# Two layer norms in a row as one function, in a two-layer attention and MLP kernel with its backward pass

## The chip, the cores and the metric

The kernel runs on one core of a Trainium2 chip. The metric is the device time of one execution in microseconds (us); lower is better. A core has five engines that run side by side: PE (TensorE, matmuls and transposes), DVE (VectorE), ACT (ScalarE), POOL (GpSimd) and SP (SyncE, which here issues most loads). They wait for each other through semaphores. Data moves between HBM and the core's memories on 16 DMA engines.

## The reference

Forward pass of four blocks over a state `x` of shape 2 x 1 x 1024 (batch 2, one token), and the gradient of all inputs but `B_x`. The weights are shared by the two layers.

```
_layernorm(x): (x - mean) / sqrt(var + 1e-5)

x = x + A(_layernorm(x))     # attention: q = y @ wq, 32 query heads, 4 kv heads, a cache
                             # of 16384 keys and values of 128, softmax, @ wo
x = x + B(_layernorm(x))     # B(x): y = _layernorm(x); gelu(y @ w1 + b1) @ w2 + b2
x = x + A(_layernorm(x))
x = x + B(_layernorm(x))
outputs: x, and d/d(x, k_cache, v_cache, wq, wo, w1, b1, w2, b2) for a given grad_out
```

B normalizes its input again, so the input of each MLP goes through two layer norms in a row: y1 = LN(x), y2 = LN(y1). wq is 1024 x 4096, wo 4096 x 1024, w1 1024 x 3584, w2 3584 x 1024; k_cache and v_cache hold 2 x 4 x 16384 x 128 bf16 values each.

## The kernel before

**Layout.** A state vector lies as `[128, 8, 2]` (1024 = 8 x 128, and the batch of two), so a layer norm sums first along the free dimension on DVE and then over the 128 partitions with a PE matmul against a matrix of ones (`part_sum`, L187 to L190). The order of the work is written out by hand in the kernel's code; each engine runs its own instructions strictly in that order.

**Loads.** Weights and cache come in tiles of 1 MB, `[128, 4096]` bf16, into a pool `ld` of seven buffers. SP issues a load when the buffer it goes to has been read to the end; SP's loads stand in one queue, in program order.

**Forward MLP** (`mlp_hidden`): `ln_fwd` twice, a copy to bf16 (`m_all`), then `w_fwd` over w1 (L337, into the PSUM bank `ACCT`), then gelu. `ln_fwd` takes the power -0.5 on POOL (L225).

**Backward MLP** (`weights_down`, for layer 1 and then layer 0). It multiplies by w1 transposed, goes backward through the two layer norms, and multiplies by wo transposed:

- `Back` is a product with a transposed weight. Some rows of the weight (the first `nd` blocks of 128) are turned on DVE (`turn32`, L269) and multiplied by `products` (L296) into a bank `..._d`; the others are turned on PE in *units* of eight 128 x 128 transposes (`turn`, L358, tiles `wtp` in a PSUM pool of two) with one copy by ACT back over the weight (L159), and multiplied at L418 into a bank `..._p`. `columns` (L305, L308) turns the `_d` bank into columns `_f`. `banks` takes both banks from the pool `ps_x` of four and clears them on DVE (L394, L397), `open` spreads the input gradient over the partitions with PE (`spg`, L278) and DVE (L281), `run` goes through the eight tiles, `some(k, n)` emits n units of tile k.
- In `weights_down`, `w1b` (banks `dm_d`, `dm_p`) is followed by `wob` (banks `do_d`, `do_p`). Seven loads of wo are emitted at once; the eighth, and SP's loads behind it, wait until the product of wob's first tile (L418 `do_p`) has released a buffer. While the layer norms run backward, PE is given units of wob's first two tiles, eight units in all, emitted through the hooks of `ln_bwd`: `hook` stands ahead of the partition sum, `after` behind it.

```
        wob.banks()
        dn = ln_bwd(dm[:], sv["y2"][:], sv["rstd2"][:], "dn", lambda: None, lambda: some(2))
        dx = ln_bwd(dn[:], sv["y1"][:], sv["rstd1"][:], "dx", lambda: some(2), lambda: some(3))
        ...
        wob.open(gA_all[:, 0:DJ, lsl(l)])
        some(8)
        wob.run()
```

So PE's order is: partition sum `lb_ps`, four units, partition sum, three units, `spg`, one unit, then the products.

**Around it.** `weights_down(1)` is followed by the attention backward of layer 1; `weights_down(0)` by the last stage, in which all gradients of the caches and weights are made and stored (`kv_pair` L1336, `dw_units` L1250, stores issued by POOL at L1213, loads by SP at L1282). `ACCT` is not in use during `weights_down`.

Of the kernel before, what the change touches and what calls it, by code (L numbers as in the profile page):

```python
# [10 lines left out]
F32 = mybir.dt.float32  # L11
I32 = mybir.dt.int32
ACT = mybir.ActivationFunctionType
ALU = mybir.AluOpType
# [5 lines left out]
LN_EPS = 1e-5  # L20
# [3 lines left out]
def kernel(  # L24
# [25 lines left out]
    V = nc.vector  # L50
# [3 lines left out]
    B, _, D = A_x.shape  # L54
# [6 lines left out]
    DJ = D // 128  # L61
# [14 lines left out]
    WIDE = 32  # L76
# [17 lines left out]
    def pt(shape, dtype, name):  # L94
        return ps_tp.tile(shape, dtype, name=name, tag="tp")

    def px(shape, dtype, name):
        return ps_x.tile(shape, dtype, name=name, tag="x")

    def pa(shape, dtype, name):  # L100
        return ps_acc.tile(shape, dtype, name=name, tag="acc")
# [31 lines left out]
    ACCT = pa([128, 512], F32, "acc_all")  # L133
# [11 lines left out]
    def copies_on(e):  # L145
        only["e"] = e
        load["A"] = load["D"] = 0.0
# [25 lines left out]
    def bcast_j(ap2, J):  # L173
        return ap2.unsqueeze(1).to_broadcast([128, J, 2])
# [12 lines left out]
    def part_sum(src, n, name):  # L187
        ps = pm_([128, n], F32, name)
        PE.matmul(ps[:], lhsT=onesf[:], rhs=src, start=True, stop=True)
        return ps  # L190
# [15 lines left out]
            V.tensor_copy(out=row[:, j0 * 128:(j0 + 4) * 128], in_=ps[0:2, :, :].rearrange("p a b -> p (a b)"))  # L206
        queue.dma_start(dram_out, row[:, :])

    def ln_fwd(xT, name):
        s1 = small.tile([128, 2], F32, name="ln_s1")  # L210
        V.tensor_reduce(out=s1[:], in_=xT.rearrange("p j b -> p b j"), axis=AX.X, op=ALU.add)
        ps = part_sum(s1[:], 2, "ln_ps")
        negmu = small.tile([128, 2], F32, name="ln_negmu")
        V.tensor_scalar(out=negmu[:], in0=ps[:], scalar1=-1.0 / D, scalar2=None, op0=ALU.mult)
        xc = wrk.tile([128, DJ, 2], F32, name="ln_xc")
        V.tensor_tensor(out=xc[:], in0=xT, in1=bcast_j(negmu[:], DJ), op=ALU.add)
        sq = wrk.tile([128, DJ, 2], F32, name="ln_sq")
        V.tensor_tensor(out=sq[:], in0=xc[:], in1=xc[:], op=ALU.mult)
        s2 = small.tile([128, 2], F32, name="ln_s2")
        V.tensor_reduce(out=s2[:], in_=sq[:].rearrange("p j b -> p b j"), axis=AX.X, op=ALU.add)  # L220
        ps2 = part_sum(s2[:], 2, "ln_ps2")
        vpe = small.tile([128, 2], F32, name="ln_vpe")
        V.tensor_scalar(out=vpe[:], in0=ps2[:], scalar1=1.0 / D, scalar2=LN_EPS, op0=ALU.mult, op1=ALU.add)
        rstd = vec.tile([128, 2], F32, name=name + "_rstd")
        nc.gpsimd.tensor_tensor(out=rstd[:], in0=vpe[:], in1=neghalf[:], op=ALU.pow)  # L225
        y = vec.tile([128, DJ, 2], F32, name=name + "_y")
        V.tensor_tensor(out=y[:], in0=xc[:], in1=bcast_j(rstd[:], DJ), op=ALU.mult)
        return y, rstd

    def ln_bwd(dy, y, rstd, name, hook=lambda: None, after=lambda: None):  # L230
        t1 = wrk.tile([128, DJ, 2], F32, name="lb_t1")
        V.tensor_tensor(out=t1[:], in0=dy, in1=y, op=ALU.mult)
        s = small.tile([128, 2, 2], F32, name="lb_s")
        V.tensor_reduce(out=s[:, 0, :], in_=dy.rearrange("p j b -> p b j"), axis=AX.X, op=ALU.add)
        V.tensor_reduce(out=s[:, 1, :], in_=t1[:].rearrange("p j b -> p b j"), axis=AX.X, op=ALU.add)
        hook()
        ps = part_sum(s[:].rearrange("p a b -> p (a b)"), 4, "lb_ps")
        after()
        nm = small.tile([128, 2, 2], F32, name="lb_nm")
        V.tensor_scalar(out=nm[:].rearrange("p a b -> p (a b)"), in0=ps[:], scalar1=-1.0 / D, scalar2=None,  # L240
                        op0=ALU.mult)
        u = wrk.tile([128, DJ, 2], F32, name="lb_u")
        V.tensor_tensor(out=u[:], in0=y, in1=bcast_j(nm[:, 1, :], DJ), op=ALU.mult)
        V.tensor_tensor(out=u[:], in0=u[:], in1=dy, op=ALU.add)
        V.tensor_tensor(out=u[:], in0=u[:], in1=bcast_j(nm[:, 0, :], DJ), op=ALU.add)
        dx = wrk2.tile([128, DJ, 2], F32, name=name, tag="lb_dx")
        V.tensor_tensor(out=dx[:], in0=u[:], in1=bcast_j(rstd, DJ), op=ALU.mult)
        return dx
# [112 lines left out]
    class Back:  # L361
# [26 lines left out]
                if self.todo[k]:  # L388
                    self.todo[k].popleft()()

        def banks(self):
            if self.nd:
                self.acc = px([128, 512], F32, self.name + "_d")
                V.memset(self.acc[:, 0:32 * self.nd], 0.0)  # L394
            if self.np:
                self.p = px([128, self.np, WIDE], F32, self.name + "_p")
                V.memset(self.p[:], 0.0)  # L397

        def open(self, gT):
            self.gT = gT  # L400
# [383 lines left out]
    def cols4(J, name, used=True):  # L784
        t = vec.tile([128, J + 7, 4], BF16, name=name)
        V.memset(t[:, (J if used else 0):J + 7, :], 0.0)
        return t[:]
# [5 lines left out]
    m_all = cols4(DJ, "m_all")  # L793
# [5 lines left out]
    saved = {}  # L799
    ALLG = list(range(G))  # L800

    def lsl(l):
        return slice(2 * l, 2 * l + 2)
# [18 lines left out]
        return xn  # L822

    def mlp_hidden(l, xT):
        y1, rstd1 = ln_fwd(xT[:], f"m{l}a")
        y2, rstd2 = ln_fwd(y1[:], f"m{l}b")
        V.tensor_copy(out=m_all[:, 0:DJ, lsl(l)], in_=y2[:])
        hps = w_fwd(B_w1, D, F, m_all[:, 0:DJ, lsl(l)])
        hpre = vec.tile([128, FJ, 2], F32, name=f"hpre{l}")
        V.tensor_tensor(out=hpre[:], in0=hps, in1=b1T[:].to_broadcast([128, FJ, 2]), op=ALU.add)  # L830
        x2 = wrk.tile([128, FJ, 2], F32, name="g_x2")
        V.tensor_tensor(out=x2[:], in0=hpre[:], in1=hpre[:], op=ALU.mult)
        w_ = wrk.tile([128, FJ, 2], F32, name="g_w")
        V.tensor_scalar(out=w_[:], in0=x2[:], scalar1=GELU_A, scalar2=1.0, op0=ALU.mult, op1=ALU.add)
        u = wrk.tile([128, FJ, 2], F32, name="g_u")
        V.tensor_tensor(out=u[:], in0=w_[:], in1=hpre[:], op=ALU.mult)
        z = wrk.tile([128, FJ, 2], F32, name="g_z")
        S.activation(out=z[:], in_=u[:], func=ACT.Exp, scale=2.0 * GELU_C)
        V.tensor_scalar(out=z[:], in0=z[:], scalar1=1.0, scalar2=None, op0=ALU.add)
        rz = wrk.tile([128, FJ, 2], F32, name="g_rz")  # L840
        V.reciprocal(out=rz[:], in_=z[:])
        th = vec.tile([128, FJ, 2], F32, name=f"th{l}")
        V.tensor_scalar(out=th[:], in0=rz[:], scalar1=-2.0, scalar2=1.0, op0=ALU.mult, op1=ALU.add)
        hh = wrk.tile([128, FJ, 2], F32, name="g_hh")
        V.tensor_scalar(out=hh[:], in0=th[:], scalar1=1.0, scalar2=0.5, op0=ALU.add, op1=ALU.mult)
        V.tensor_tensor(out=h_all[:, 0:FJ, lsl(l)], in0=hh[:], in1=hpre[:], op=ALU.mult)
        saved[f"m{l}"] = dict(y1=y1, rstd1=rstd1, y2=y2, rstd2=rstd2, hpre=hpre, th=th, xT=xT)

    def mlp_out(l, fps):
        xn = vec.tile([128, DJ, 2], F32, name=f"xM{l}")  # L850
# [25 lines left out]
    def weights_down(l, gT, name, mid=None):  # L876
        sv = saved[f"m{l}"]
        w1b = Back(B_w1, D, F, 4, [1, 0, 3, 2, 5, 4, 6], "dm")
        for k in range(len(w1b.tiles)):
            w1b.load(k)  # L880
        w1b.banks()
        w1b.open(dh_all[:, 0:FJ, lsl(l)])
        copies_on("A")
        w1b.some(0)
        w1b.run(mid)
        wob = Back(A_wo, HD, D, 16, [4, 5, 0, 1, 6, 2, 3, 7], "do")
        for k in range(NLD):
            wob.load(k)
        w1b.columns()
        dm = wrk.tile([128, DJ, 2], F32, name="dm_sb")  # L890
        for (p, ap), e in zip(w1b.parts(), (V.tensor_copy, S.copy)):
            e(out=dm[:, p], in_=ap)
        q = deque([(0, 0), (0, 0), (0, 0), (0, 0), (1, 0), (1, 0), (1, 0), (1, 0)])

        def some(n):
            for _ in range(n):
                if q:
                    wob.some(q.popleft()[0], 1)

        wob.banks()  # L900
        dn = ln_bwd(dm[:], sv["y2"][:], sv["rstd2"][:], "dn", lambda: None, lambda: some(2))
        dx = ln_bwd(dn[:], sv["y1"][:], sv["rstd1"][:], "dx", lambda: some(2), lambda: some(3))
        gn = vec.tile([128, DJ, 2], F32, name=f"gM{l}")
        V.tensor_tensor(out=gn[:], in0=dx[:], in1=gT[:], op=ALU.add)
        V.tensor_copy(out=gA_all[:, 0:DJ, lsl(l)], in_=gn[:])
# [3 lines that stand above are left out]
        wob.columns()  # L909
        copies_on(None)  # L910
        return gn, wob.parts()
# [174 lines left out]
    banks = {"tp": lambda: pt([128, 8, 128], BF16, "tpe")}  # L1086
# [423 lines left out]
    m = 0  # L1510
    while 2 * m < NS + 2:
# [7 lines left out]
        for k in range(2):  # L1519
            s = 2 * m + k  # L1520
            if s < NS:
                i, b = NCH + s // NB, s % NB
# [97 lines left out]
```

## Time and profile before

| | |
|---|---|
| time, median of 3 runs | 1140.46 us (1137.77 to 1141.27) |
| profiled execution: its own time / its span | 1139.88 us / 1138.1 us |
| busy, of the span: PE, DVE, ACT, POOL | 80%, 54%, 47%, 6% |
| moved by DMA | 449.20 MB, mean 395 GB/s |
| layer norms of `mlp_hidden`, from the first reduction to `m_all` | 207.1 to 214.2 us (layer 0), 428.3 to 435.7 us (layer 1) |
| `weights_down` from `dm_sb` to the first `do_p` product | 468.8 to 477.4 us (layer 1), 709.8 to 718.4 us (layer 0) |

Positions are us from the start of the span. In the stage tables ("windows"), the columns after the stretch are its length, then busy time and number of instructions of PE, PEld (weight loads), DVE, ACT and POOL, then the granted PE clock (1.00 is full speed), the busy share of the 16 DMA engines, and GB/s. In the chain of waits, each piece is what the piece after it waited for.

### The profile page before, as it was taken

How to read it: one execution, taken by the hardware profiler on the slowest of the kernel's cores; microseconds unless marked ns; L12 is line 12 of the kernel's file. 1: busy time of each engine (PE TensorE's matmuls, PEld its weight loads, DVE VectorE, ACT ScalarE, POOL GpSimd, SP SyncE). 2: the span in 40 equal slices, each digit the busy share in tenths (PEclk: the TensorE clock that was granted, in tenths of full speed). 3: DMA queues.
4: the chain of work that ended last, by engine and by line, in shares of the span. 5: the costliest groups of instructions: out<-in, count | busy, mean ns of one | idle time of the engine just before them, and what ended most of it. 6: DMA issues, size and time to landing. Idle time of an engine off the chain costs nothing.

```text
span 1138.1 us, 38123 instructions
## 1 busy us (share of the span) xinstructions
PE 915.9 (80%) x16766; PEld 674.7 (59%) x16767; DVE 619.8 (54%) x1363; ACT 534.0 (47%) x1356; POOL 70.2 (6%) x124
## 2 busy tenths in 40 slices
PE   4979795468888975789887678888898897899996
PEld 3867674358766754778765567755545454455552
DVE  1545451180545523654442246678798767786876
ACT  0544351005544420434333214468697766676764
POOL 0000000000000000000000000022121111111210
PEclk9988895567999875899998678999999978897978
DMA  8999999999999979999999699998999999999997
GB/s 371 423 425 425 424 424 413 395 413 423 423 425 423 412 288 404 388 422 421 399 413 393 232 380 309 370 386 302 403 419 421 421 419 424 423 411 421 423 385 290
DMA packets 104183, 449.20 MB, mean 395 GB/s; under 512 B 7238, under 2 KB 11334, under 8 KB 66896
## 3 DMA queue, kind: packets, MB, share of 16 engines
q1 hardware_dynamic: 86672, 354.46, 77.6%
q0 software_dynamic: 17344, 92.29, 19.6%
q8 instruction: 131, 2.15, 0.7%
q14 instruction: 36, 0.29, 0.1%
HBM read 348.14 MB, written 98.58 MB: 393 GB/s over the span
## 4 chain that ended last, share of the span: by engine, by line
PE 45%; DMA 35%; DVE 10%; issue 5%; ACT 4%; POOL 0%; SPq 0%; DVEq 0%; ACTq 0%; POOLq 0%
DMA kv_V<-in_A_v_cache_dram 13%; PE tp L480 10%; DMA wt<-in_B_w_dram 5%; PE acc_all L512 4%; PE tpm L1527 4%; DMA kv_K<-in_A_k_cache_dram 4%; PE xm L1336 4%; DMA wt<-in_A_wo_dram 3%; DMA out_dram<-keepK 3%; DMA keepK<-in_A_v_cache_dram 3%; PE sc L633 3%; PE xm L1250 2%; PE wtp L358 2%; PE dp L1389 2%; PE dp L726 2%
## 5 line engine op out<-in xcount | busy, mean ns | idle before, releaser
L159 ACT COPY kT<-tp 128x512 int32<-128x512 int32 x200 | 117.4, 587 | 298.4 <-PE tp L480 289.1
L162 DVE COPY kT<-tp 128x1024 bf16<-128x1024 bf16 x168 | 114.9, 690 | 141.8 <-PE tp L480 130.4
L480 PE MATMUL tp<-ident,kv_K 128*128 128x128 bf16 x1728 | 142.0, 230 | 6.9 <-DMA kv_K<-in_A_k_cache_dram 6.8
L480 PEld LDWEIGHTS <-kv_K 128*128 128x128 bf16 x1728 | 107.8, 103 | 7.7 <-DMA kv_K<-in_A_k_cache_dram 7.5
L170 DVE CAST big<-xm 128x512 bf16<-128x512 f32 x133 | 86.3, 684 | 19.3 <-PE xm L1336 14.3
L167 ACT CAST big<-xm 128x512 bf16<-128x512 f32 x151 | 82.1, 595 | 25.0 <-PE xm L1336 14.8
L633 PE MATMUL sc<-qT_bf,kT 128*128 128x8 bf16 x2048 | 91.5, 171 | 0.1
L633 PEld LDWEIGHTS <-kT 128*128 128x128 bf16 x2048 | 75.7, 97 | 26.7 <-issue 20.8
L337 PEld LDWEIGHTS <-wt 128*128 128x128 bf16 x1920 | 57.4, 104 | 54.7 <-issue 17.8
L167 ACT CAST keepV<-xm 128x512 bf16<-128x512 f32 (+1 forms) x137 | 75.0, 594 | 29.5 <-PE xm L1336 18.5
L480 PE MATMUL tp<-ident,kv_V 128*128 128x128 bf16 x864 | 70.2, 227 | 14.1 <-DMA kv_V<-in_A_v_cache_dram 12.2
L597 ACT ACTIVATE e_all<-sc,negm 128x64 bf16<-128x64 f32 x256 | 77.2, 343 | 1.0 <-DVE negm L592 1.0
L170 DVE CAST keepV<-xm 128x512 bf16<-128x512 f32 (+1 forms) x101 | 65.9, 684 | 18.9 <-PE xm L1336 12.7
L269 DVE STREAM_TRANSPOSE wt<-wt 128x512 int32<-128x512 int32 x104 | 63.6, 674 | 14.2 <-PE w2b_f L337 11.0
L512 PE MATMUL acc_all<-kv_V,e_all 128*16 128x256 bf16 x864 | 46.0, 293 | 28.7 <-DMA kv_V<-in_A_v_cache_dram 14.4
L159 ACT COPY wt<-wtp 128x512 int32<-128x512 int32 x72 | 40.3, 587 | 57.0 <-PE wtp L358 54.1
L480 PEld LDWEIGHTS <-kv_V 128*128 128x128 bf16 x864 | 55.2, 101 | 16.2 <-DMA kv_V<-in_A_v_cache_dram 13.1
L597 ACT ACTIVATION_READ_ACCUMULATOR e_all<-sc,negm 128x1 f32 x256 | 59.8, 234 | 0.0
L167 ACT CAST keepK<-xm 128x512 bf16<-128x512 f32 x98 | 53.0, 596 | 14.1 <-PE xm L1336 7.5
L1389 PE MATMUL dp<-wdo,kT 128*128 128x64 bf16 x896 | 52.8, 206 | 0.0
L358 PE MATMUL wtp<-ident,wt 128*128 128x128 bf16 x576 | 47.8, 244 | 4.9 <-ACT wt L159 2.6
L1336 PE MATMUL xm<-QmK,blk 64*128 64x512 bf16 x256 | 48.8, 444 | 2.3 <-ACT keepV L167 1.0
(387 smaller groups left out, 1564.4 us busy)
## 6 DMA issues: line engine op xcount, KB each, us to landing
kv_K<-in_A_k_cache_dram SPq DMA_DIRECT2D x81, 1024.0 KB, 13.0
kv_V<-in_A_v_cache_dram SPq DMA_DIRECT2D x81, 1024.0 KB, 12.9
wt<-in_B_w_dram SPq DMA_DIRECT2D x42, 1024.0 KB, 12.9
wt<-in_A_wo_dram SPq DMA_DIRECT2D x32, 1024.0 KB, 9.6
out_dram<-big POOLq DMA_DIRECT2D x26, 1024.0 KB, 18.9
out_dram<-keepV POOLq DMA_DIRECT2D x19, 1024.0 KB, 20.7
out_dram<-keepK POOLq DMA_DIRECT2D x17, 1024.0 KB, 17.8
wt<-in_A_wq_dram SPq DMA_DIRECT2D x16, 1024.0 KB, 11.0
```

The source lines that it names most:

```text
L159: S.copy(out=dst.bitcast(I32), in_=src.bitcast(I32))
L162: V.tensor_copy(out=dst, in_=src)
L167: S.copy(out=dst, in_=src)
L170: V.tensor_copy(out=dst, in_=src)
L269: V.transpose(out=w, in_=w)
L358: PE.transpose(tp[:, o, :], view[:, o * 128:(o + 1) * 128], ident[:])
L480: PE.transpose(tp[:, j, :], cv[:, b * 8 + j, :], ident[:])
L512: PE.matmul(self.acc[cg:cg + 16, :], lhsT=coef(u), rhs=self.cv[:, t:t + 2, :].rearrange("p t d -> p (t d)"), start=False, stop=True, tile_ ...
L597: S.activation(out=e_all[:, g, f * half:(f + 1) * half, l, h, :], in_=sc[g][f][:, h, :].rearrange("p (a b) -> p a b", b=2), func=ACT.Exp, ...
L633: PE.matmul(sc[g][f][:, :, t % TH], lhsT=kT[:, j, :], rhs=q_bf[:, g, :], start=True, stop=True)
L1336: PE.matmul(pss[k][:], lhsT=blk[p:p + 64, o + 2 * h + k // 2, :], rhs=Qm[p:p + 64, :, :].rearrange("p a b -> p (a b)"), start=True, stop=T ...
L1389: PE.matmul(dp[:, :, t:t + 4], lhsT=kT[:, j, :], rhs=wd[:, :, x:x + 4], start=(b + j == 0), stop=False)
```

## The change

With m = mean, v = variance of x, the second norm sees mean 0 and variance v/(v+eps), so LN(LN(x)) = (x - m) / sqrt(v(1+eps) + eps^2). `ln_fwd` and `ln_bwd` get a flag `twice` for this formula and its gradient, and `mlp_hidden` and `weights_down` call them once in place of twice. One addition in `ln_bwd` becomes a `scalar_tensor_tensor` for all callers. The bank `dm_p` is no longer taken from the pool of four; it lies in `ACCT`. `wob.banks()` stands ahead of `w1b.columns()`. Of the eight wo units, two are emitted ahead of the only `ln_bwd`, four behind its partition sum, and the last two behind `spg`.

```diff
-    def ln_fwd(xT, name):
+    def ln_fwd(xT, name, twice=False):
...
-        V.tensor_scalar(out=vpe[:], in0=ps2[:], scalar1=1.0 / D, scalar2=LN_EPS, op0=ALU.mult, op1=ALU.add)
+        V.tensor_scalar(out=vpe[:], in0=ps2[:], scalar1=(1.0 + twice * LN_EPS) / D,
+                        scalar2=LN_EPS ** 2 if twice else LN_EPS, op0=ALU.mult, op1=ALU.add)
...
-    def ln_bwd(dy, y, rstd, name, hook=lambda: None, after=lambda: None):
+    def ln_bwd(dy, y, rstd, name, hook=lambda: None, after=lambda: None, twice=False):
...
-        V.tensor_tensor(out=u[:], in0=u[:], in1=dy, op=ALU.add)
+        V.scalar_tensor_tensor(out=u[:], in0=u[:], scalar=1.0 + twice * LN_EPS, in1=dy, op0=ALU.mult, op1=ALU.add)
...
-        def banks(self):
+        def banks(self, p_home=None):
...
-                self.p = px([128, self.np, WIDE], F32, self.name + "_p")
-                V.memset(self.p[:], 0.0)
+                self.p = p_home[:, 0:self.np * WIDE].rearrange("p (j b) -> p j b", b=WIDE) if p_home is not None else px(
+                    [128, self.np, WIDE], F32, self.name + "_p")[:]
+                V.memset(self.p, 0.0)
...
     def mlp_hidden(l, xT):
-        y1, rstd1 = ln_fwd(xT[:], f"m{l}a")
-        y2, rstd2 = ln_fwd(y1[:], f"m{l}b")
-        V.tensor_copy(out=m_all[:, 0:DJ, lsl(l)], in_=y2[:])
+        y, rstd = ln_fwd(xT[:], f"m{l}", True)
+        V.tensor_copy(out=m_all[:, 0:DJ, lsl(l)], in_=y[:])
...
     def weights_down(l, gT, name, mid=None):
-        w1b.banks()
+        w1b.banks(ACCT)
         w1b.open(dh_all[:, 0:FJ, lsl(l)])
         copies_on("A")
         w1b.some(0)
         w1b.run(mid)
         wob = Back(A_wo, HD, D, 16, [4, 5, 0, 1, 6, 2, 3, 7], "do")
         for k in range(NLD):
             wob.load(k)
+        wob.banks()
         w1b.columns()
         dm = wrk.tile([128, DJ, 2], F32, name="dm_sb")
...
-        q = deque([(0, 0), (0, 0), (0, 0), (0, 0), (1, 0), (1, 0), (1, 0), (1, 0)])
+        q = deque([0] * 4 + [1] * 4)
...
-        wob.banks()
-        dn = ln_bwd(dm[:], sv["y2"][:], sv["rstd2"][:], "dn", lambda: None, lambda: some(2))
-        dx = ln_bwd(dn[:], sv["y1"][:], sv["rstd1"][:], "dx", lambda: some(2), lambda: some(3))
+        some(2)
+        dx = ln_bwd(dm[:], sv["y"][:], sv["rstd"][:], "dx", lambda: None, lambda: some(4), True)
```

## The prediction

> **What bounds the kernel.** I read the page's chain first, then the two stretches the change touches, forward and backward.
>
> ```profile
> PE 45%; DMA 35%; DVE 10%; issue 5%; ACT 4%; POOL 0%; SPq 0%; DVEq 0%; ACTq 0%; POOLq 0%
> ```
>
> PE and DMA share the path, so a saved instruction counts only where its own stage waits for it. Forward, the timeline of layer 0's norms and the stage table over them:
>
> ```profile
> 210.36 0.17 DVE L227 TENSOR_TENSOR m0a_y<-ln_xc,m0a_rstd 128x16 f32<-128x16 f32 x1 [0.81 <-POOL m0a_rstd L225]
> 213.84 0.17 DVE L227 TENSOR_TENSOR m0b_y<-ln_xc,m0b_rstd 128x16 f32<-128x16 f32 x1 [0.80 <-POOL m0b_rstd L225]
> 214.86 3.63 PE L337 MATMUL acc_all<-m_all,wt 128*128 128x18 bf16 x128 [2.02 <-DVE acc_all L345]
> 220.02 0.93 PEld L337 LDWEIGHTS <-wt 128*128 128x128 bf16 x32 [1.63 <-DMA wt<-in_B_w_dram]
> ```
> ```profile
> 207.50:210.00 2.50, 0.98 (x4) 0.81 (x4) 0.84 (x5) 0.00 (x0) 0.36 (x1) 0.50 1.04 400
> 210.00:212.50 2.50, 0.83 (x4) 0.75 (x5) 1.02 (x6) 0.00 (x0) 0.32 (x1) 0.50 1.06 407
> 212.50:215.00 2.50, 0.48 (x8) 0.42 (x9) 0.98 (x4) 0.00 (x0) 0.69 (x1) 0.50 1.04 395
> ```
>
> The DMA column never falls below 1.04. When the norms end, PE takes four waiting tiles in 3.63 us and then waits for loads again.
>
> Backward, the chain of waits in `weights_down(0)`:
>
> ```profile
> 710.30 0.50 DVE do_d L394
> 710.84 0.48 DVE do_p L397
> 711.75 0.35 PE lb_ps L189 x2
> 712.40 0.52 PE wtp L358 x6
> 712.99 0.59 ACT wt L159
> 713.63 1.52 PE wtp L358 x16
> 715.15 0.33 PE lb_ps L189 x2
> 715.47 2.35 PE wtp L358 x24
> 718.45 7.23 DVE wt L269 x12
> ```
>
> Here the norms are on the path, but mostly through the transposes that PE does between them. The stage table, cut where the clock changes:
>
> ```profile
> 468.20:471.60 3.40, 1.62 (x31) 1.52 (x32) 1.96 (x9) 0.17 (x1) 0.00 (x0) 0.51 1.05 407
> 707.20:710.65 3.45, 2.28 (x99) 1.84 (x95) 1.62 (x5) 1.24 (x3) 0.00 (x0) 1.00 0.86 287
> 710.65:714.05 3.40, 1.87 (x26) 1.60 (x27) 2.12 (x13) 1.06 (x2) 0.00 (x0) 1.00 1.00 359
> 714.05:717.45 3.40, 3.40 (x35) 3.40 (x33) 1.21 (x7) 1.99 (x5) 0.00 (x0) 0.50 1.05 401
> ```
>
> After a stretch with PE busy 1.87 of 3.40 the clock (third column from the end) stood at half; after one with 2.28 of 3.45 it stayed full. And layer 1's DMA hole:
>
> ```profile
> 479.00:479.50 0.50, 0.24 (x10) 0.21 (x7) 0.50 (x2) 0.00 (x0) 0.00 (x0) 1.00 0.58 225
> 479.50:480.00 0.50, 0.00 (x0) 0.00 (x0) 0.50 (x2) 0.00 (x0) 0.00 (x0) 1.00 1.55 242
> 480.00:480.50 0.50, 0.47 (x32) 0.43 (x31) 0.50 (x2) 0.00 (x0) 0.00 (x0) 1.00 0.69 168
> 480.50:481.00 0.50, 0.50 (x20) 0.42 (x9) 0.50 (x2) 0.00 (x0) 0.00 (x0) 1.00 0.46 172
> ```
>
> **Forward part.** Each layer loses seven DVE instructions, two partition sums and one POOL power: 213.84 - 210.36 = 3.48 us in layer 0, 435.00 - 431.52 = 3.48 in layer 1 (timeline). I cost both at nothing: loads running at DMA share 1.04 to 1.06 (1.05 in layer 1, 427.5 to 440) hide them, and the wait at 220.02 would only begin earlier. Without that cover they would be worth 7.0 us. The new scalars in `vpe` cost nothing.
>
> **Small backward edits.** `dm_p` in `ACCT` has the same memset (0.165 us) and copy (0.166 us), and nobody else holds the bank. A `scalar_tensor_tensor` of 128x64 takes 0.225 us, a `tensor_tensor` 0.216: three of them, nothing.
>
> **Memsets.** `do_d` and `do_p` (0.50 + 0.48) leave the chain at 710.30. They now stand on DVE between the last `Gw`, which ends at 708.83, and `xt`, which starts at 709.34 when PE is done. Two at a pitch of 0.54 end near 709.90, so `xt`, queued behind them, and `dm_f` and `dm_sb` come 0.56 late. `lb_t` follows `dm_sb` (710.03) at the usual pitch of 0.21: 710.24 + 0.56 = 710.80 in place of 711.23. Net gain 0.43. In layer 1 the places are the same (`Gw` ends 467.73, `xt` 468.24).
>
> **Units and the one norm, layer 0.** Eight DVE instructions and one partition sum go, but what counts is PE's order: two units, `lb_ps`, four units, `spg`, two units. Tiles are there: wob's first tiles were issued from 693.79 and DMA stood idle (25 GB/s at 706.0 to 706.5) before they were needed.
> - `dm_f` ends at 709.96 + 0.56 = 710.52. Two units at full clock, 0.55 each (16 transposes in 1.09): 711.62. `lb_ps`, ready at 711.32, waits for them, and DVE's `lb_nm` behind it; it ends at 711.97.
> - Four units at ACT's pace of 0.64 (two per 1.28, as 690.29 to 691.59): 714.53.
> - Meanwhile DVE needs 1.44 from `lb_ps` to `gA_all` (715.48 to 716.92 before): 713.41. So what is late next is the transposes, not the norm.
> - `spg` at 714.55 instead of 717.76: 3.2 earlier. DVE's turns of wt follow by 0.69 as before, at 715.25 instead of 718.45, and the chain runs through them (7.23 us).
> - The last two units now stand ahead of the first `do_p` product: 714.55 + 0.27 + 1.28 = 716.1 instead of 718.41, 2.3 earlier, so SP's eighth wo load and the loads behind it go out 2.3 earlier. DMA lost about 2.4 us in its hole here (328, 74, 49, 49, 106, 82 and 233 GB/s in the half microseconds from 718.5 against 405).
>
> After this stage the chain holds no DMA until 837, so the whole 3.2 should pass. Were PE at half clock throughout (unit 0.85, `lb_ps` 0.53): 710.52 + 1.70 + 0.53 + 3.40 = 716.15, gain 1.6. I take full clock, because the stretch from 710.65 then has PE busy some 3 of 3.40 us, more than the 2.28 that kept it.
>
> **Layer 1.** Here the clock is already at half from 468.2. `dm_f` ends at 468.94 + 0.57 = 469.51, two units 471.21, `lb_ps` 471.77, four units 475.17: `spg` 1.6 earlier than 476.81, first product at 475.17 + 0.27 + 1.28 = 476.7 instead of 477.42, 0.7 earlier. Were the clock full from 471.6, the four units would end at 474.3, and these gains become 2.5 and 1.6. But the next stage is fed by DMA at 421 to 423 GB/s from 484 to 540, so I count only the hole that the earlier eighth load closes: 185 + 168 + 242 + 238 GB/s short of 410 over half a microsecond each, 1.0 us in all, closed by 0.7 to 1.0: 0.9. If PE sets the pace there (busy 19.3 of 20 us, 500 to 520), up to 2.5.
>
> The Trainium skill (TensorE: Matmul & The Clock Gate, "What's actually happening") has the clock released after one busy window of a free-running 3.4 us. The rows agree in that steps lie 3.4 us apart. By that rule layer 1 would go to full clock at 471.6, its hole would close fully, and the sum would be 4.2 instead of 4.1; were layer 0 nevertheless to stay at half clock, it would be 2.5.
>
> **Sum.** 0 + 3.2 + 0.9 = 4.1 us. On the profiled execution's own 1139.88: 1135.8. That one lies 0.58 under the median of the runs, so on 1140.46: **1136.4**. Ends of the unknown costs: 0.7 + 1.6 = 2.3 (1138.2), and 2.5 + 3.2 = 5.7 (1134.8).
>
> **Rivals.**
> - *Half clock in both layers* (10%): transposes stay slow and, six units ahead of `spg`, eat most of what the norm gives: 1138.2. For it: the drop at 714.05. Against: PE's hole of 1.8 us at 710, which caused it, is filled.
> - *Swallowed later* (11%): from 837 on loads wait for stores and DMA runs at 420 GB/s; layer 0's gain is lost there and 0.9 remains: 1139.6. Against: DMA runs at only 347, 288 and 259 GB/s in the stretches from 760 to 790, waiting for compute, which starts earlier.
> - *Slower: the last stage falls into another order of stores* (13%). SP's loads at L1282 wait 125.2 us in all for stores of `big` and 78.8 for `keepK`; the chain has a store of 17.66 us at 885 and a load of 23.98 at 932. If the shift lets more 1 MB stores slip ahead of loads that the chain needs, each costs 1.05 MB / 0.42 = 2.5 us. From two slips on the gain is gone; four give +5.9: 1146.4. For it: POOL's and SP's issues meet there by time alone. Against: program order is unchanged in that stage.
> - *Forward was not hidden* (6%): another 7.0: 1129.4. Against: the DMA column.
>
> **Numbers.** The forecast has 60%. A measurement of this kernel can tell about 0.3%, 3.4 us, from no change: faster means below 1137.0, slower above 1143.9. Faster: the forecast but for 4 in 60, and the last rival: 0.62. Same: those 4, half clock, swallowed: 0.25. Slower: 0.13. The range goes from 1133.8, a little past the largest bound, to 1142.0, past the swallowed case.
>
> **What would show it.** Right: one `ln_ps` pair fewer per MLP, PE still waiting for w1 loads after 214, hpre unmoved; PE transposing at once after `dm_f`; clock full from 710 to 717; `spg` following the sixth unit, 2.5 to 3.3 us sooner after the last `Gw` in layer 0; both DMA holes smaller. Wrong: hpre earlier by 3 us (forward counts); half clock in the units; a stage from 837 to the end longer than before by some us, with longer waits of L1282 for stores.

## The result and the profile after

The changed kernel took **1136.29 us** (median of 20 runs, 1131.84 to 1141.93) against 1140.33 for the kernel before (20 runs beside it): ratio 0.9968, 95% interval 0.9954 to 0.9982. The medians differ by 4.0 us; by the interval it is 2 to 5 us less. The forecast was 1136.4. The sum was met. Its largest term, as the rest of this text shows, was not.

Single runs of one kernel scatter by 2 to 4 us (standard deviation), so a difference of two profiled executions is no measure of the change. The profiled one of the changed kernel has an own time of 1131.86 us (span 1130.0), 4.4 under its median. Only distances inside a stage are compared below.

The page of the changed kernel, busy time and instructions, the instruction queue (packets, MB, share of the 16 DMA engines), and the chain:

```profile
PE 914.7 (81%) x16755; PEld 676.1 (60%) x16755; DVE 614.5 (54%) x1333; ACT 533.1 (47%) x1356; POOL 68.7 (6%) x122
q8 instruction: 131, 2.15, 0.7%
PE 50%; DMA 30%; DVE 10%; ACT 4%; issue 4%; POOL 0%; SPq 0%; ACTq 0%; DVEq 0%; POOLq 0%
```

The second line looked like nothing and turned out to be the key. PE's products and weight loads are 2 x 16,755 instructions; divided by the 131 packets of 16.4 KB that is 256 a packet. So nearly all of these packets must be TensorE's own code, 256 instructions at a time.

**Forward.** The timeline of layer 0 after the change:

```profile
210.24 0.17 DVE L228 TENSOR_TENSOR m_y<-ln_xc,m_rstd 128x16 f32<-128x16 f32 x1 [0.81 <-POOL m_rstd L226]
211.26 1.89 PE L338 MATMUL acc_all<-m_all,wt 128*128 128x18 bf16 x64 [2.02 <-DVE acc_all L346]
214.66 0.93 PEld L338 LDWEIGHTS <-wt 128*128 128x128 bf16 x32 [1.60 <-DMA wt<-in_B_w_dram]
```

The products start 3.6 us sooner (211.26 for 214.86). But PE finds two tiles in place of four, and then waits 1.60 us for the next load, as it does for each one behind it. `hpre`, the end of the stage, is at 226.21 us (226.36 before) in layer 0 and at 446.64 (446.07) in layer 1.

**Backward, layer 0.** The timeline, from the last `Gw` to the end of wo's products:

```profile
704.73 0.29 DVE L282 TENSOR_TENSOR Gw<-spg,strip 128x128 bf16<-128x128 f32 x1 [0.82 <-PE spg L279]
...
705.13 0.48 DVE L395 MEMSET do_d<- 128x512 f32 x1
705.67 0.48 DVE L399 MEMSET do_p<- 128x512 f32 x1
706.06 0.28 DVE L306 STREAM_TRANSPOSE xt<-dm_d 128x128 f32<-128x128 f32 x1
...
706.59 1.07 PE L359 MATMUL wtp<-ident,wt 128*128 128x128 bf16 x16
707.51 0.36 PE L189 MATMUL lb_ps<-lb_s,onesf 128*128 128x4 f32 x2
...
710.23 0.27 PE L279 MATMUL spg<-gA_all,ident 128*32 128x16 bf16 x16
...
719.16 0.28 PE L420 MATMUL do_p<-gA_all,wt 128*128 128x32 bf16 x5 [1.36 <-issue]
...
725.10 0.28 PE L420 MATMUL do_p<-gA_all,wt 128*128 128x32 bf16 x5 [1.39 <-issue]
```

The two memsets stand ahead of `xt`, PE transposes at once after `dm_f`, and `spg` starts 5.5 us after the last `Gw` (at 704.73) where it took 9.2 before. The last two lines are new: PE pauses 1.36 and 1.39 us with no recorded cause ("issue"), in the middle of a run of products, 5.94 us apart. The kernel before had one such pause there, of 0.64 us. Its lines for the same stage:

```profile
708.54 0.29 DVE L281 TENSOR_TENSOR Gw<-spg,strip 128x128 bf16<-128x128 f32 x1 [0.84 <-PE spg L278]
...
717.76 0.27 PE L278 MATMUL spg<-gA_all,ident 128*32 128x16 bf16 x16
...
730.41 0.58 PE L418 MATMUL do_p<-gA_all,wt 128*128 128x32 bf16 x17 [0.64 <-issue]
```

**Layer 1's DMA hole.** Two of the half microseconds that were shown with 225 and 242 GB/s:

```profile
479.00:479.50 0.50, 0.50 (x29) 0.38 (x18) 0.50 (x2) 0.00 (x0) 0.00 (x0) 1.00 1.13 410
479.50:480.00 0.50, 0.50 (x13) 0.50 (x10) 0.50 (x2) 0.04 (x1) 0.00 (x0) 1.00 0.97 360
```

The hole is closed, as expected.

### The profile page after: what moved, and what is told of

Read it like the earlier page. It is cut to its first block, busy times and chain, and to the rows that moved or that the text cites. A ratio compares the mean times of both kernels' runs of the same rounds, so it can differ in the third digit from the quotient of the medians.

```text
span 1130.0 us, 38068 instructions
## 1 busy us (share of the span) xinstructions
PE 914.7 (81%) x16755; PEld 676.1 (60%) x16755; DVE 614.5 (54%) x1333; ACT 533.1 (47%) x1356; POOL 68.7 (6%) x122
## 4 chain that ended last, share of the span: by engine, by line
PE 50%; DMA 30%; DVE 10%; ACT 4%; issue 4%; POOL 0%; SPq 0%; ACTq 0%; DVEq 0%; POOLq 0%
PE tp L482 11%; DMA kv_V<-in_A_v_cache_dram 10%; DMA wt<-in_B_w_dram 5%; PE acc_all L514 5%; PE tpm L1528 5%; PE xm L1337 4%; DMA wt<-in_A_wo_dram 4%; DMA kv_K<-in_A_k_cache_dram 4%; PE sc L635 3%; PE xm L1251 3%; PE wtp L359 3%; PE dp L1390 2%; DMA keepK<-in_A_v_cache_dram 2%; DMA out_dram<-keepK 2%; PE dp L728 2%
## 5 line engine op out<-in xcount | busy, mean ns | idle before, releaser
L482 PE MATMUL tp<-ident,kv_K 128*128 128x128 bf16 x1728 | 147.2, 235 | 5.2 <-DMA kv_K<-in_A_k_cache_dram 5.2
L482 PEld LDWEIGHTS <-kv_K 128*128 128x128 bf16 x1728 | 111.9, 105 | 5.9 <-DMA kv_K<-in_A_k_cache_dram 5.8
L482 PEld LDWEIGHTS <-kv_V 128*128 128x128 bf16 x864 | 55.5, 102 | 14.5 <-DMA kv_V<-in_A_v_cache_dram 13.3
L170 DVE CAST keepK<-xm 128x512 bf16<-128x512 f32 x69 | 44.7, 683 | 8.8 <-PE xm L1337 4.2
## 6 DMA issues: line engine op xcount, KB each, us to landing
kv_V<-in_A_v_cache_dram SPq DMA_DIRECT2D x81, 1024.0 KB, 12.3
```

Of the source, the lines that this page charges most:

```text
L170: V.tensor_copy(out=dst, in_=src)
L482: PE.transpose(tp[:, j, :], cv[:, b * 8 + j, :], ident[:])
```

## The experiments

The question was which of the three parts (forward, backward in layer 1, backward in layer 0) brings the 4.0 us. The theory was the prediction's: 0, 0.9 and 3.2. Two rivals were that the forward part counts, and that layer 0's gain is lost again; a third came up later, that TensorE's own code comes too late. Each was timed beside the kernel before, on the same chip. Where an old backward function meets the combined forward one, it gets the combined y for both norms and a tile of ones for the second 1/std.

**Backward alone.** The forward pass takes the two norms in turn again:

```diff
-        y, rstd = ln_fwd(xT[:], f"m{l}", True)
+        y1, rstd1 = ln_fwd(xT[:], f"m{l}a")
+        y, rstd2 = ln_fwd(y1[:], f"m{l}b")
+        rstd = vec.tile([128, 2], F32, name=f"m{l}_rstd")
+        V.tensor_tensor(out=rstd[:], in0=rstd1[:], in1=rstd2[:], op=ALU.mult)
```

> The changed kernel, but the forward pass computes the two norms one after the other as before (and multiplies their two 1/std for the one backward norm, one small DVE instruction). Theory (forward is hidden by the loads of w1): the whole gain stays, about -4.1 us against the kernel before (ratio 0.996); hpre within 1 us of before in both layers; spg of wo about 1.6 us (layer 1) and 3.2 us or more (layer 0) sooner after the last Gw. Rival (the forward norms count): the gain shrinks by 3.5 us per layer, to nothing or a loss of up to 3 us.

Measured: 1138.80 us against 1140.69, ratio 0.9971 [0.9947, 0.9996]. The backward half alone brings about 3 us (0.5 to 6), which agrees with the whole change and does not exclude a part for the forward half.

**Forward alone, twice.** The kernel before with the combined forward norm:

```diff
-        saved[f"m{l}"] = dict(y1=y1, rstd1=rstd1, y2=y2, rstd2=rstd2, hpre=hpre, th=th, xT=xT)
+        saved[f"m{l}"] = dict(y1=y, rstd1=rstd, y2=y, rstd2=onesf[:, 0:2], hpre=hpre, th=th, xT=xT)
```

> The kernel before, with the combined norm in the forward pass alone; the two backward norms and the places and order of units stay as they were (both get the combined y, and the second norm's 1/std is a tile of ones, which changes the gradient slightly). Theory: no change, within 1 us (ratio 0.999 to 1.001); first w1 product 3.5 us sooner after xA, hpre unmoved within 0.5 us. Rival (the forward norms count): -4 to -7 us (ratio 0.994 to 0.9965).

> The kernel before with the forward half of the change alone, once more (its old backward form gets the combined y in both places and a tile of ones for the second 1/std). Theory that the saving of the forward pass is hidden behind the loads of w1: the ratio to before lies at 1.000, and the first run's 0.9979 was the spread of the runs. Rival that the forward half gives about 2 us in another way: 0.998 again. In the trace both expect hpre of layer 0 within 0.3 us of before's 226.36.

Measured: 1138.40 against 1140.69, 0.9979 [0.9963, 0.9996]; again 1138.31 against 1139.89, 0.9984 [0.9967, 1.0002]. In the traces `hpre` of layer 0 is at 226.55 and 226.06 us, of layer 1 at 446.07 and 446.44: unmoved within 0.4. So the stage itself gives nothing, as forecast, and yet the total is about 2 us lower, twice. Neither interval alone excludes the 0.999 to 1.001 of the first theory; the two together speak against 1.000. Where these 2 us come from is open.

**One layer's backward alone.** The old `weights_down` is called for the other layer, with the combined forward pass in both:

```diff
-    g1, dops = weights_down(0, g2, "0", lambda: (col_to_row_f32(x4, DJ, out_0.rearrange("b s d -> (b s) d"), "o0"),
+    g1, dops = weights_down_two(0, g2, "0", lambda: (col_to_row_f32(x4, DJ, out_0.rearrange("b s d -> (b s) d"), "o0"),
```

> The changed kernel, with the backward part of the change in layer 1 alone; layer 0 keeps two backward norms, its memsets and its unit order as before (the second norm's 1/std a tile of ones). Theory: -0.9 us (ratio 0.999), lead of 1.3 us at the start of layer 1's attention backward, about 0 to 1 us of it left at 600 us. Rival (layer 1's earlier end is worth much more later, in the thin DMA stretch 620 to 660): -3 to -4 us, with a lead of 3 us or more at 660.

> The changed kernel, with the backward part of the change in layer 0 alone; layer 1 keeps its two backward norms, memsets and unit order (the second norm's 1/std a tile of ones). Theory: -3.2 us (ratio 0.997), spg of wo 3.2 to 3.7 us sooner after the last Gw of layer 0, and that lead carried to the end. Rival (swallowed in the store-bound last stage, the gain seen in the total comes from layer 1): within 1 us of before.

Measured: with layer 1's alone 1136.91, 0.9960 [0.9942, 0.9979]; with layer 0's alone 1140.45, 1.000 [0.998, 1.002]. Both theories (0.999 and 0.997) lie outside the intervals, and both rivals' totals inside. Both kernels also hold the forward half. So layer 0's backward part, the largest term of the sum, brings nothing that can be seen. A least-squares fit of the three parts to the differences of the means in these five runs and the two of the whole change, each weighted by its scatter, gives forward -2.0, layer 1 -2.4 and layer 0 +0.8 us, each within 1.0 to 1.5; the single runs lie up to 1.4 us off it.

Inside the stages, the distance from the last `Gw` to `blocks` (DVE's operation behind `spg`), from there to the copy of `do_p` into `dof`, and the sum, in us:

| layer 0 | to `blocks` | to `dof` | sum | pauses of 0.25 us or more behind `spg` |
|---|---|---|---|---|
| before | 9.57 | 13.23 | 22.80 | 0.64 |
| forward alone, two runs | 8.20, 8.19 | 13.43, 12.92 | 21.63, 21.11 | 0.82, 0.32 |
| layer 1 alone (layer 0 old) | 9.22 | 12.91 | 22.13 | 0.30 |
| changed, two runs | 5.85, 5.84 | 15.16, 16.45 | 21.01, 22.29 | 2.75, 2.84 |
| backward alone | 5.84 | 16.17 | 22.01 | 3.89 |
| layer 0 alone | 5.84 | 17.73 | 23.57 | 4.11 |

The new order gains 2.4 to 3.7 us up to `blocks`, every time, and gives 1.7 to 4.8 back behind it. This is where the expected gain went. Of the 3.7 us against the kernel before, 1.4 go with the clock: in the two forward-alone traces the old order had full clock too, and took 8.2 us in place of 9.57.

**Shifted code.** To see whether the pauses belong to places in the code, 64 tiny products at the start of the kernel before move everything behind them by 128 instructions:

```diff
+    pad = pm_([128, 2], F32, "pad")
+    for _ in range(64):
+        PE.matmul(pad[:], lhsT=ident[:], rhs=ident[:, 0:2], start=True, stop=True)
```

> The kernel before with 64 tiny matmuls more (128 PE instructions) at the very start, where PE waits for its first load: all of PE's later code is shifted by half of a 256-instruction block. Theory (PE pauses where a 256-instruction block of its code ends and the DMA engines are full): the pauses without a recorded cause move by 128 instructions, their number stays 8 to 10, and the total stays within 1.5 us of before (ratio 0.9985 to 1.0015). Rival (where the blocks end is worth several us, and the -2.4 us of the forward-only kernel came from its code being four instructions shorter): a change of 2 us or more in either direction.

Measured: 1138.19 against 1139.21, 0.9981 [0.9958, 1.0004]. In layer 0 the pause of 0.64 us left its place, 15 products into the last `do_p` run, and one of 0.81 us stands 64 products, 128 instructions, earlier, inside a transpose unit. So the pauses belong to places in TensorE's code. They lie 256 instructions apart: the fourteen traces have 80 pauses of TensorE of 0.8 us or more without a recorded cause between 440 and 830 us, and counted from the start of the trace the first product behind each stands at place 194 or 195 of a block of 256. The trace of the shifted code has seven such pauses in all, where 8 to 10 were expected. The ratio lies between theory and rival and excludes neither: a shift of the code alone may be worth up to 0.4%.

**Two units fewer ahead of spg** (`some(2)` for `some(4)` behind the partition sum):

> The changed kernel with two units instead of four behind the partition sum, so that two of them move behind spg (order: two, sum, two, spg, four). Theory (in layer 0 PE waits for code behind spg, so an earlier spg is given back there): spg 1.0 to 1.3 us sooner after the last Gw (about 4.7 us instead of 5.8), the stretch from spg to the first dof longer by as much, total as the changed kernel within 1 us (ratio 0.996 to 0.9975). Rival (the chain of DVE's turns behind spg carries the gain, as predicted): another 1 to 2 us, ratio 0.995 or less.

Measured: 1137.26, 0.9982 [0.9961, 1.0004]. `blocks` came 4.99 us after the last `Gw`, 0.85 sooner still, and `dof` 17.13 after that: the sum, 22.12, is that of the other orders. The rival's 0.995 is excluded. In this trace it doesn't matter which unit stands ahead of `spg`; the end of the stage is set by something else.

**The changed kernel again:**

> The changed kernel once more, for a second trace and more runs. Both theories: ratio 0.997. If the pauses behind spg belong to the change, layer 0 shows 5.8 us from the last Gw to spg, 2 to 4 us of pauses behind it and 15 us or more from spg to dof, against 9 us and 13 us before; if they were chance, 13 us and under 1 us of pauses.

Measured: 1135.35, 0.9980 [0.9954, 1.0006]; a pause of 2.32 us ahead of the first `x5` products, where the first trace had 1.36, and again 5.94 us from there to the second. Ahead of the second it is only 0.22 us, since the granted clock was at half in between (0.50 from 723.6 to 727.1) and TensorE itself took 5.7 us for the block. So the pauses belong to the change and were not chance.

**What the pauses wait for.** Cut into windows of a quarter of a microsecond, the DMA view of the changed kernel shows TensorE's code on its way, among the loads. First 716.50 to 716.75 us, then 722.75 to 723.00 (packets and rate; instruction queue: packets, MB, share of 16 engines):

```profile
DMA packets 46, 0.11 MB, mean 434 GB/s; under 512 B 0, under 2 KB 0, under 8 KB 45
q8 instruction: 1, 0.02, 23.1%
...
DMA packets 37, 0.12 MB, mean 483 GB/s; under 512 B 0, under 2 KB 0, under 8 KB 31
q8 instruction: 1, 0.02, 24.1%
```

One packet takes 0.231 x 16 x 0.25 = 0.92 us. The pauses ended at 719.16 and 725.10, 2.4 and 2.3 us after these packets began (716.73 and 722.76). In all 80 pauses a packet of this queue had begun 2.2 to 2.7 us before TensorE went on. And a packet starts late when the DMA engines are full: after the boundary at 719.16 the next one started 3.6 us later, with 416 GB/s moving; with the engines idle it was 1.1 us (below). Over all boundaries of the fourteen traces between 440 and 830 us the packet came 0.5 us later (median of 17, at most 1.2) where under 50 GB/s moved until then, and 3.0 us later (median of 497) at 400 GB/s or more. So 256 instructions take 3.6 + 2.3 = 5.9 us here, the 5.94 seen from pause to pause (5.9 to 8.0 in the other traces with the new order), while TensorE issues such a block in 4.6 (two turns of 16 transposes, 64 `do_d` and 27 + 5 `do_p` products: 719.16 to 723.72).

In the kernel before the engines had a hole just then. The window from 720 to 722 us, before and after:

```profile
720.00:722.00 2.00, 1.21 (x49) 1.06 (x46) 2.00 (x4) 0.00 (x0) 0.00 (x0) 1.00 0.46 118
```
```profile
720.00:722.00 2.00, 1.73 (x29) 1.61 (x30) 0.52 (x1) 1.17 (x3) 0.00 (x0) 1.00 1.03 434
```

Before, at 118 GB/s, a packet of code started at 720.1 us and no pause followed. The changed kernel has no such hole at the same distance from its last `Gw` either (406 GB/s from 716.2 to 718.2). The change closed it, and with it the gap through which the code came.

**One block of code more.** 128 products of two columns behind the third tile's products in layer 0 (`wob.run` calls them after `prod(2)`):

```diff
+        def filler():
+            if l == 0:
+                pad = pm_([128, 512], F32, "pad")
+                for _ in range(128):
+                    PE.matmul(pad[:, 0:2], lhsT=ident[:], rhs=ident[:, 0:2], start=True, stop=True)
-        wob.run()
+        wob.run(filler)
```

> The changed kernel with 128 matrix products of two columns (256 instructions of TensorE with their weight loads, one block of code) added in layer 0 only, behind the third tile's wo products. Products of this size lasted 27 ns each (64 of them from 1.4 to 3.1 us in the run with shifted code), so they are 3.5 us of TensorE's time. Theory that TensorE, behind spg, waits for its own instructions: with the DMA queues full a block of 256 takes 5.94 us from pause to pause, so the way from the blocks to the last do_p grows by about 5.9 us, with one pause more, and each pause ends 2.3 to 2.6 us after a packet of the instruction queue begins to move. Rival that TensorE's work or the turns of VectorE bound this way: it grows by at most 3.5 us and the pauses stay as they were or shrink. Total: about 1141.5 (theory) or 1137 to 1139 (rival).

Measured: 1141.30 us, 1.0017 [0.9993, 1.0041], 5.0 above the changed kernel. From `blocks` to `dof` it took 19.91 us, 4.75 more than the first trace of the changed kernel and 3.5 more than the second. So the total fits the theory; the stage lies between the two and does not settle it. The forecast of one pause more missed: there is one, of 2.85 us. The next packet of code again started 3.4 us after the boundary, at 406 GB/s, but the clock stood at half (0.50 from 721.7 to 728.6), TensorE took 6.2 us for that block, and the code was there in time.

**Long products.** The same hook after `prod(2)` and `prod(5)`, with six products of 512 columns at each place, so that TensorE gets work but hardly any code:

```diff
+                for _ in range(6):
+                    PE.matmul(pad[:].rearrange("p (a b) -> p a b", b=256), lhsT=ident[:],
+                              rhs=blocks8[:].unsqueeze(1).to_broadcast([128, 2, 256]), start=True, stop=True)
```

> The changed kernel with six matrix products of 512 columns added behind the third tile's wo products in layer 0 and six more behind the sixth's: 12 instructions at each place with their weight loads, and about 0.21 us each by the granted clock (6 times 0.21 is 1.3 us at each place, 2.6 in all). Theory that TensorE waits for its own instructions: the pauses of about 1.4 us before the last five do_p shrink by what is added, and the way from the blocks to the last do_p grows by under 0.7 us. Rival that TensorE's work bounds it: it grows by 2.6 us and the pauses stay. Total: within 1 us of the changed kernel (theory), or 2.6 us more (rival).

Measured: 1135.60 us, 0.9968 [0.9942, 0.9995], the changed kernel's own ratio. Its timeline:

```profile
721.53 0.43 PE L420 MATMUL do_p<-gA_all,wt 128*128 128x32 bf16 x11 [0.34 <-issue]
...
722.45 1.47 PE L913 MATMUL pad<-blocks,ident 128*128 128x512 bf16 x6
...
727.75 0.58 PE L420 MATMUL do_p<-gA_all,wt 128*128 128x32 bf16 x17 [0.51 <-issue]
```

Two times 1.47 us of work were added, the pauses shrank to 0.34 and 0.51, and `blocks` to `dof` took 15.87: 0.7 us more than in the changed kernel's first trace, 0.6 less than in its second, for 2.9 us of TensorE's time. The four traces of the same order without added products have 15.16 to 17.73 us and 2.8 to 4.1 us of pauses. So TensorE's work does not bound this stretch; the wait for its code does.

**Held loads, twice.** A tiny transfer that waits for DVE holds SP's queue in layer 0, so that the six loads behind wob's eighth start later and the engines fall idle for TensorE's code:

```diff
         wob.run()
+        if l == 0:
+            hold = vec.tile([128, 2, 2], F32, name="hold")
+            V.memset(hold[:, 0], 0.0)
+            nc.sync.dma_start(hold[0:1, 1], hold[0:1, 0])
         wob.columns()
```

> The changed kernel with the six loads behind wob's eighth load held on SP in layer 0 until DVE has done its last turn (a tiny transfer on SP that waits for a memset behind the turns), about 7 us later than now; this opens a hole of some 4 us in DMA there. Theory (code): pauses behind spg in layer 0 under 1 us in all, spg to dof 13.4 us or less, so the last stage starts 2 to 3 us sooner after spg; the total 1 to 2 us below the changed kernel (ratio 0.995 to 0.996), since DMA has slack at 760 to 790. Rival (DMA is what bounds, the pauses are not its doing): pauses stay, the total rises by 2 to 4 us over the changed kernel (ratio 0.999 to 1.000).

> The changed kernel with the loads behind wob's eighth held back in layer 0, once more. Theory that the held loads leave the queue free for TensorE's next block of code: the pause at the second boundary behind the first do_p is gone again, and the time is 1 to 2 us under the changed kernel's 1136.3 (first run 1134.3). Rival that what the pause gives is taken back by the later loads: the same time as the changed kernel within 1 us.

Measured: 1134.28, 0.9953 [0.9929, 0.9978]; again 1134.97, 0.9951 [0.9926, 0.9976]. Against the kernel before this is the best of all versions, 1 to 2 us under the changed kernel; the intervals overlap, so that this last step isn't shown. What was expected of the stage in the first run missed: its pauses behind `spg` sum to 2.85 us (under 1 expected), and `blocks` to `dof` took 16.03 (13.4 or less). In the second run it is 1.48 and 14.87. What both traces lack is the pause ahead of the last products. The timeline of the second run:

```profile
720.12 0.28 PE L420 MATMUL do_p<-gA_all,wt 128*128 128x32 bf16 x5 [1.48 <-issue]
...
720.93 3.51 PE L359 MATMUL wtp<-ident,wt 128*128 128x128 bf16 x32
...
724.94 0.97 PE L420 MATMUL do_p<-gA_all,wt 128*128 128x32 bf16 x32
```

The first pause stays, since its code was fetched while wob's own tiles came in (3.8 us after its boundary, at 403 GB/s). Then the engines fall idle (10 GB/s from 720 to 722), the next packet starts at 721.2, 1.1 us after the boundary, and `x32` products run through without the second pause. The middle line may be a second price of a pause: these 32 transposes took 3.51 us where the changed kernel's first trace has 2.4 for the two pairs. The granted clock was 0.70 and 0.50 (720 to 722, 722 to 724), after a stretch with PE busy 0.64 of 2 us (718 to 720). The half clock helped to hide the second pause, as in the changed kernel's second trace, so the hole in the loads is not its only cause.

## Why the prediction was right, and where it was not

- **Forward, 0.** In its stage right: the wait for w1 loads begins sooner, `hpre` stays. In the total it brought about 2 us in both runs. The step "loads hide them" holds up to 446 us; that nothing else would follow from it was not seen to be true. A code shift of 128 instructions alone gave 0.9981, and the forward half makes TensorE's code 16 instructions shorter (16,759 weight loads for 16,767, each with its product; the recorded "four instructions" is too few). So places of code may account for it, and so may the granted clock; neither is shown.
- **Memsets, 0.43.** Right: the two stand between the last `Gw` and `xt`, which starts 0.53 us later after `Gw` (forecast 0.56), and `lb_t` comes 0.43 sooner after it.
- **Clock and units in layer 0.** Right. The clock stayed at 1.00 from 705 to 732 us in the changed kernel's trace, so the rival with half clock fell. `spg` came 3.7 us sooner (forecast 3.2), with four units in 2.3 us where 2.56 were assumed. But PE's busy time by itself does not tell when the clock falls: it fell behind a stretch of 1.87 us in 3.40 in the kernel before, and stayed at 1.00 behind one of 1.78 in 3.41 (709.63 to 713.04) in the first forward-alone trace.
- **"The whole 3.2 should pass."** This step failed. It was argued from the chain, which held no DMA there until 837 us. But TensorE's code moves on the same DMA engines, and the chain puts a wait for it down to nothing or to "issue". Behind `spg` TensorE needs a new block for every 256 instructions, 5.94 us or more each with the engines full. The sooner the eighth load and the six behind it go out, the fuller they are. So what was late next was neither the turns of wt nor the norm, but the instructions. Layer 0's stage took 22.18 us on average in the five traces with the old order and 22.22 in the four with the change's own order (21.94 with two units fewer and the two with held loads taken in; single traces 20.7 to 23.6). Nothing of the 3.2 can be seen.
- **Layer 1, 0.9.** The mechanism is right for the changed kernel's first trace: half clock up to `spg`, which came 1.9 us sooner (forecast 1.6), the first product 1.3 sooner (0.7), the hole closed; full clock came back at 475.9. Half clock up to `spg` holds in only four of the nine traces with the new order; in the others the clock came back a window sooner or had not fallen, and the first product came 1.9 us sooner on average. In the stage the sum fell from 22.9 us (five traces) to 22.0 (nine): 0.9. In the total the fit gives 2.4 within 1.5, near the upper bound of 2.5 that was worked out for a pace set by PE. From the last `Gw` of layer 1 to that of layer 0 the same traces average 240.2 us with the old order and 238.4 with the new, 1.8 less, but single ones differ by up to 5. How 0.9 in the stage becomes more in the end isn't shown.
- **The sum.** 4.1 forecast, 4.0 measured, out of 0 + 0.9 + 3.2 forecast and about 2.0 + 2.4 - 0.8 by the fit. The hit is luck for the larger part: the gain that layer 0 lost was made up from places that the prediction held at nothing or at less. A slip beside the sum: with layer 0 at half clock and layer 1's hole fully closed, its own terms give 1.0 + 1.6 = 2.6, not 2.5.
- **The rivals.** "Swallowed later" was right that layer 0's gain is lost, and wrong on the place: not behind 837 us, but within 15 us of `spg`. The slower case needs a stage from 837 us on that is longer by some us; the ratio excludes it for the total. "Forward was not hidden" needs `hpre` sooner; it stayed.

The Trainium skill (Runtime: NRT & Kernel Launch, "Instruction fetch mechanics") says that an engine's code is refilled in blocks of 16 KiB, 256 instructions, through a DMA queue of its own, and that this is mostly hidden, since an engine dispatches more slowly than the code arrives. The size agrees with the 131 packets of 16.4 KB. Over the whole kernel "mostly hidden" holds: the pauses of 0.8 us or more are eight in the changed kernel's first trace, 12.3 us in all, 1.1% of the span (before: nine, 13.3 us). Beside full DMA it does not hold for TensorE: behind `spg` a block was issued in 4.6 us and the next one took 5.9 to arrive.

## What to carry to other kernels

Before crediting a gain on TensorE where it issues many short instructions, count them: here, where 256 of them passed in less than some 6 us beside full DMA, it waited for its code, and reordering the work gained nothing. Fewer instructions or a gap in the loads are what could help; held loads are the one such try here, and their gain in the total isn't shown. A filled DMA hole is not always a gain, for something unseen may have used it. And a total that fits is no evidence for its terms; run each part alone.

## What was not expected of the hardware

- TensorE's code competes with the loads: a packet of 256 instructions started 1.1 us after the boundary with idle engines and 3.6 us with 416 GB/s moving (medians over the traces 0.5 and 3.0), and TensorE went on 2.2 to 2.7 us after its start, in 80 pauses of 80.
- Time and granted clock go together from run to run: over the 20 runs of the changed kernel the correlation with the mean granted clock is -0.59, with 3.6 us less for each 0.01 of it; over 35 runs of the kernel before -0.58 and 3.0. The mean clock was 0.8533 and 0.8506. That is about a third of the scatter's variance. Whether the clock makes the time, or waits make both, isn't shown.
